# Moving the gate, the subtractions and the order of products in the head of a gated attention kernel

## The chip, the cores and the metric

The kernel runs on one core of a Trainium2 chip. The metric is the device time of one execution in microseconds; the time before is 2952.81 us, the median of three runs (2950.8 to 2952.96). The engines are called TensorE (PE in the profile), VectorE (DVE), ScalarE (ACT), GpSimd (POOL) and SyncE (SP), which issues nearly all DMA transfers from one queue in program order.

## The reference

For one sequence x of 2048 rows and 1024 columns, in fp32, with 32 heads of 32 columns:

```python
g = sigmoid((x * gate_w).sum(-1, keepdims=True))
a = linear_attention(x, A_wqkv, A_wo)      # phi(q), phi(k); num / den; @ wo
b = softmax_attention(x, B_wqkv, B_wo)     # softmax(q k^T / sqrt(32)) v; @ wo
return g * a + (1 - g) * b
```

Each attention begins with `x @ wqkv`, a 2048 x 1024 by 1024 x 3072 product. The gate `g` is one number for each row of x.

## The kernel before, in words

**Precision.** TensorE multiplies fp32 operands as a rounded high part and a remainder. `split` (L292) makes both: ScalarE copies the source to the high part (L293), and an engine given by the caller subtracts the high part from the source (L294). `three` (L148) then issues three matmuls (L152, L155, L157) for each pair of operands: high by high, and the two mixed ones.

**The head** is everything ahead of `linear()`. It computes the q, k and half of the v of the softmax attention, in two passes J over halves of the sequence. One pass has two parts.

*v.* `v_pass` (L397) goes over eight steps k of the contraction and adds 24 matmuls a step into all eight PSUM banks. The loop at L573 (pass 0) and the one at L629 (pass 1) feed it: x and weight tiles of 128x512 are loaded and split (`split_x`, `split_wv`). At the end `v_out` (L355) has ScalarE copy the eight banks to SBUF buffers (L356) and SyncE store them.

*q and k.* For these the kernel takes seven products instead of eight for a 2x2 block product (a Strassen-Winograd scheme). `sides` (L370) forms sums of x tiles, `split_sides` and `last_side` split them; `quad_weights` (L418) forms and splits seven weight combinations from four raw tiles. `quad` (L444) runs one group: seven products of 12 matmuls each into six banks taken in turn (`NQB`, `turns`), and combinations of them on VectorE (L468 to L482), which read the banks and leave four results. Each result is split by `store` (L458) and sent to DRAM (`qk_d`). There are eight groups in a pass (`QUADS`). `PRODUCTS` gives their order: X11, X21, X22 are pieces of x itself, T1 to T4 are sums; `PLACE` says which big buffers hold each.

**Order of work.** Within the head the program order is written out by hand: between two products `next(side)` advances several generators (`beside`, L505): the next group's weights one step, the late T4 splits (`late_side`), the spill of split x to DRAM (`spill_rest`), and one piece of the gate (`gate`, L491). Each engine runs its instructions in this order. A gate piece is a load of 128 rows by 256 columns of x into `kvb`, which is the only buffer for it, and a VectorE multiply with a sum (L497); there are 64, four for each of 16 row tiles. `leave` (L675), in the last group, begins the loads of the next stage.

**After the head**, `linear()` (L930) makes units of 24 matmuls: first the second half of v (16 units, one for each 128 rows), with x read back from DRAM (`load_half`), then the linear attention's k, v and q. A planner at L1637 interleaves the units with the softmax attention's heads by modelled engine times (`T`, `use`); row maxima of the first heads (L1126, L1131) run beside the second half of v. The weights of the next projection are split towards the end of a stage (`renew`, `split_w`: ScalarE L729, VectorE L731). From the heads on GpSimd adds up softmax rows (L1392).

Of the kernel before, what the change touches and what calls it, by code (L numbers as in the profile page):

```python
# [10 lines left out]
F32 = mybir.dt.float32  # L11
F32R = mybir.dt.float32r
AF = mybir.ActivationFunctionType
ALU = mybir.AluOpType
# [33 lines left out]
def kernel(  # L48
# [260 lines left out]
    PLACES = [dict(zip(SIDE, PLACE)), dict(zip(["X11", "T4", "X21", "X22", "T1", "T2", "T3"], PLACE))]  # L309
    for side in PLACES:  # L310
        side["X12"] = side["T4"]
    PRODUCTS = ["X11", "T1", "T2", "X21", "T3", "X22", "T4"]
# [37 lines left out]
    H11, H22, H12, H21, P1, U2, W2, C22 = mid[6], mid[7], mid[8], mid[9], mid[2], mid[10], mid[11], mid[12]  # L350
# [19 lines left out]
    def sides(raws, i):  # L370

        r11, r12, r21, r22 = raws
        nc.gpsimd.tensor_sub(r11, r12, r11)
        nc.gpsimd.tensor_sub(r12, r22, r12)
        nc.gpsimd.tensor_sub(r22, r22, r11)
        nc.gpsimd.tensor_sub(t4_raw[i], r21, r22)

    def split_sides(raws, J, i):
        r11, r12, _, r22 = raws
        for name, raw in (("T1", r11), ("T2", r22), ("T3", r12)):  # L380
            split(xpiece(J, name, 0, i), xpiece(J, name, 1, i), raw, nc.gpsimd)

    def last_side(J, parts):
        for i in parts:
            split(xpiece(J, "T4", 0, i), xpiece(J, "T4", 1, i), t4_raw[i], nc.vector if i % 2 else nc.gpsimd)

    def spill(J, name):

# [29 lines left out]
    def quad_weights(raws, J, f):  # L418

        w11, w12, w21, w22 = raws  # L420

        def part(s, raw, eng):
            n = quad_ring(J, f, s)
            split(ring_w(n, 0), ring_w(n, 1), raw, eng)

        part(0, w11, nc.gpsimd)
        part(6, w22, nc.vector)
        nc.vector.tensor_add(w22, w21, w22)
        nc.vector.tensor_sub(w21, w11, w21)
        yield  # L430
        part(1, w22, nc.gpsimd)
        nc.vector.tensor_sub(w11, w22, w11)
        yield
        part(3, w12, nc.gpsimd)
        part(2, w11, nc.vector)
        yield
        nc.vector.tensor_sub(w12, w12, w11)
        part(4, w21, nc.gpsimd)
        yield
        part(5, w12, nc.vector)  # L440

    turns = count()

    def quad(J, f, side):  # L444
# [12 lines left out]

        def store(i, jj, src, hi):  # L458
            split(f32r(hi), f32r(src), src, nc.gpsimd)
# [9 lines left out]
        nc.vector.tensor_add(W2, p5, U2)  # L469
        next(side, None)  # L470
        nc.vector.tensor_add(P1, product(3), P1)
        store(0, 0, P1, H11)
        next(side, None)
        p7 = product(4)
        nc.vector.tensor_add(C22, p7, W2)
        nc.vector.tensor_add(U2, p7, U2)
        store(1, 1, C22, H22)
        next(side, None)
        nc.vector.tensor_add(W2, product(5), W2)
        store(0, 1, W2, H12)  # L480
# [5 lines left out]
    GW = NK * DH  # L486
    NG = D // GW
    gate_x = kvb.rearrange("p k d -> p (k d)")
    tg = mx[0].rearrange("p t i -> p (t i)")

    def gate():  # L491
        dma(zrep, bass.AP(tensor=gate_w.tensor, offset=gate_w.offset, ap=[[0, P], [1, D]]))
        for t in range(NT):
            for i in range(NG):
                dma(gate_x, x[t * P:(t + 1) * P, i * GW:(i + 1) * GW])
                yield
                nc.vector.scalar_tensor_tensor(bank[7][:, :GW], gate_x, 1.0, zrep[:, i * GW:(i + 1) * GW],  # L497
                                               op0=ALU.mult, op1=ALU.mult, accum_out=tg[:, t * NG + i:t * NG + i + 1])
# [4 lines left out]
        nc.vector.tensor_scalar(omg_sb, g_sb, -1.0, 1.0, op0=ALU.mult, op1=ALU.add)  # L503

    def beside(*streams):  # L505

# [22 lines left out]
    for _ in range(WARM):  # L529
        nc.tensor.matmul(bank[7][:, :P], ones, ones, start=True, stop=True)  # L530

    gates = gate()
    V_BANKS = [list(range(8)), [6, 7, 2, 3, 4, 5, 0, 1]]
    raws_q = [raw_a, raw_b]

# [22 lines left out]

    def quads(J, first, spills):

        sides_ = [late_side(J), spills, gates]
        for f in range(QUADS - 1):
            if f + 2 < QUADS:
                load_quad(raws_q[f % 2], f + 2)
            else:
                first()
            quad(J, f, beside(quad_weights(raws_q[(f + 1) % 2], J, f + 1), *sides_))
# [26 lines left out]
        big[b] = big_tile(b, F32R)  # L594
    w_t[3] = big[RAW_BIG[0]]
    quad_w = quad_weights(raw_a, 0, 0)
    next(quad_w)
    next(quad_w)
    split_sides(raw_x0[3], 0, 3)
    load_quad(raw_b, 1)  # L600
    for _ in quad_w:
        pass
    for t in range(2 * TPC):
        v_out(0, t, bank[V_BANKS[0][t]], v_outs[t % 4])

    def change():

# [52 lines left out]
            for _ in quad_w:  # L660
                pass
    for t in range(2 * TPC):
        v_out(0, 2 * TPC + t, bank[V_BANKS[1][t]], v_outs[t % 4])

    def load_v1(raws, ks):
        for raw, k in zip(raws, ks):
# [252 lines left out]
        give(b, 0.0, [item])  # L919
        o_left.append(item)  # L920

    for s in [gates]:
        for _ in s:
            pass
    quad(1, QUADS - 1, leave())
    T["sp"] = 0.0
    for m in range(3):
# [1 line left out]

    def linear():  # L930
        extra = iter(())
        for n, (i, t) in enumerate(units):
            kind, c = chunks[i]
            follow = chunks[i + 1] if i + 1 < len(chunks) else None
# [787 lines left out]
```

## Time and profile before

| what | value |
|---|---|
| median of three runs | 2952.81 us |
| profiled execution | 2949.11 us, its span 2947.3 us |
| TensorE busy | 2848.4 us, 97% of the span |
| VectorE busy | 2204.3 us, 75% |
| ScalarE busy | 1598.0 us, 54% |
| GpSimd busy | 2170.3 us, 74% |
| mean granted TensorE clock | 0.984 |
| DMA | 428.57 MB, 139 GB/s of it to and from HBM |

Lines of windows give, for a stretch of the span in microseconds, its length and then the busy time of PE, of PE's weight loads, DVE, ACT and POOL (with the number of instructions), the granted PE clock, the busy share of the DMA engines and GB/s. Lines of waits give who waited for what: microseconds in total, times, longest. Lines of the timeline give start, length, engine, line, operation, and in brackets the idle time in front and what ended it. Neighbouring matmuls overlap, so a matmul's length is not the distance to the next.

### The profile page before, as it was taken

The numbers are of one execution on the slowest core, as the hardware profiler recorded it, in microseconds if no ns is written. First come the engines' busy times: TensorE is split into PE (matmuls) and PEld (weight loads), VectorE is DVE, ScalarE is ACT, GpSimd is POOL, SyncE is SP. The second block draws the span as 40 slices with busy tenths as digits, with TensorE's granted clock in tenths as the row PEclk, the third lists the DMA queues.
The fourth block names the chain that finished last, engine by engine and source line by source line (L and its number), as shares of the span: only waits on it lengthen the run. The fifth ranks groups of instructions, "written<-read, shape, count | busy, mean of one in ns | idle before, by whom it ended". The sixth has DMA issues, their size and how long they took to land.

```text
span 2947.3 us, 46931 instructions
## 1 busy us (share of the span) xinstructions
PE 2848.4 (97%) x15944; PEld 2070.4 (70%) x15944; DVE 2204.3 (75%) x3568; ACT 1598.0 (54%) x2994; POOL 2170.3 (74%) x1082
## 2 busy tenths in 40 slices
PE   8888789899999999999999999999999999999999
PEld 6667677777767767767776777777676667666787
DVE  6555465378888888888888888878887888787622
ACT  4223333046667666766676666666666666566410
POOL 7445555039999998999999999889989988886000
PEclk9889999999999999999999999999999999999999
DMA  7656675643334433433443335446666454643542
GB/s 237 208 177 205 190 221 190 208 158 101 100 98 126 110 91 98 128 101 100 106 125 91 97 99 145 141 152 192 187 182 207 130 154 121 176 117 113 198 158 79
DMA packets 383626, 428.57 MB, mean 145 GB/s; under 512 B 105774, under 2 KB 219694, under 8 KB 383388
## 3 DMA queue, kind: packets, MB, share of 16 engines
q1 hardware_dynamic: 369788, 412.47, 45.9%
q0 software_dynamic: 13600, 13.11, 3.3%
q8 instruction: 127, 2.08, 0.3%
q14 instruction: 111, 0.91, 0.1%
HBM read 298.06 MB, written 112.98 MB: 139 GB/s over the span
## 4 chain that ended last, share of the span: by engine, by line
PE 85%; DMA 4%; issue 1%; POOL 1%; DVE 1%; ACT 0%; SPq 0%; DVEq 0%; POOLq 0%; ACTq 0%
PE bank L1300 16%; PE bank L1126 16%; PE bank L1457 15%; PE bank L152 12%; PE bank L155 12%; PE bank L157 12%; DMA kvb<-in_x 2%; PE bank L1191 1%; PE bank L907 1%; DMA big<-wa 0%; PE bank L796 0%; DMA big<-wv 0%; SPq L169 0%; POOL big L294 0%; DMA big<-xs 0%
## 5 line engine op out<-in xcount | busy, mean ns | idle before, releaser
L1392 POOL TENSOR_TENSOR big<-big,big 128x512 f32<-128x512 f32 (+2 forms) x694 | 1644.7, 2374 | 118.8 <-ACT big L1303 76.1
L1131 DVE TENSOR_REDUCE mx<-bank 128x1 f32<-128x512 f32 x2048 | 1308.6, 683 | 318.5 <-PE bank L1126 314.6
L1303 ACT ACTIVATE big<-bank 128x512 f32<-128x512 f32 x2048 | 1180.2, 602 | 430.8 <-PE bank L1300 360.2
L1126 PE MATMUL bank<-big,big 128*128 128x512 f32 x1888 | 738.7, 392 | 4.8 <-DMA big<-qk 3.6
L1300 PE MATMUL bank<-big,big 128*128 128x512 f32 x1888 | 742.3, 394 | 0.5 <-ACT mid L356 0.5
L152 PE MATMUL bank<-big,big 128*128 128x512 f32 x1600 | 637.0, 398 | 73.7 <-DVE mid L469 32.7
L155 PE MATMUL bank<-big,big 128*128 128x512 f32 x1600 | 633.8, 396 | 6.4 <-POOL big L294 5.4
L157 PE MATMUL bank<-big,big 128*128 128x512 f32 x1596 | 631.0, 395 | 0.4 <-DVE big L294 0.4
L1457 PE MATMUL bank<-big,mid 128*32 128x512 f32 x4096 | 454.1, 593 | 0.0
L1300 PEld LDWEIGHTS bank<-big,big 128*128 128x128 f32 x1888 | 353.9, 188 | 126.8 <-issue 48.6
L1126 PEld LDWEIGHTS bank<-big,big 128*128 128x128 f32 x1888 | 354.3, 188 | 80.6 <-ACT big L1303 4.2
L152 PEld LDWEIGHTS bank<-big,big 128*128 128x128 f32 x1600 | 306.8, 192 | 146.7 <-issue 36.7
L155 PEld LDWEIGHTS bank<-big,big 128*128 128x128 f32 x1600 | 307.0, 192 | 72.2 <-POOL big L294 6.0
L157 PEld LDWEIGHTS bank<-big,big 128*128 128x128 f32 x1596 | 305.4, 191 | 65.7 <-DVE big L294 0.8
L1457 PEld LDWEIGHTS bank<-big,mid 128*32 128x32 f32 x4096 | 142.3, 110 | 265.5 <-issue 265.5
L1408 DVE TENSOR_TENSOR bank<-bank,big 128x512 f32<-128x512 f32 x364 | 251.8, 692 | 5.7 <-ACT big L1303 3.9
L294 POOL TENSOR_TENSOR mid<-mid,mid 128x512 fp32r<-128x512 f32 x64 | 83.4, 1304 | 164.6 <-ACT mid L293 164.5
L152 PE MATMUL bank<-big,xh 128*128 128x512 f32 x384 | 151.6, 395 | 6.4 <-DMA xh<-xs 5.6
L155 PE MATMUL bank<-big,xh 128*128 128x512 f32 x384 | 151.0, 393 | 0.7 <-DMA big<-wa 0.7
L157 PE MATMUL bank<-big,xh 128*128 128x512 f32 x384 | 150.6, 392 | 0.3 <-DMA xh<-xs 0.3
L1388 POOL TENSOR_TENSOR big<-big,big 128x1536 f32<-128x1536 f32 (+1 forms) x31 | 122.5, 3952 | 35.8 <-ACT big L1303 35.8
L293 ACT CAST mid<-mid 128x512 fp32r<-128x512 f32 x64 | 39.7, 621 | 180.1 <-issue 68.7
(129 smaller groups left out, 2111.6 us busy)
## 6 DMA issues: line engine op xcount, KB each, us to landing
big<-xs SPq DMA_DIRECT2D x300, 256.0 KB
big<-qk SPq DMA_DIRECT2D x720, 64.0 KB
xh<-xs SPq DMA_DIRECT2D x148, 256.0 KB
qk<-mid SPq DMA_DIRECT2D x128, 256.0 KB
big<-oA SPq DMA_DIRECT2D x84, 256.0 KB
xs<-big SPq DMA_DIRECT2D x64, 256.0 KB
oA<-mid SPq DMA_DIRECT2D x64, 256.0 KB
big<-big POOLq DMA_DIRECT2D x50, 256.0 KB, 5.6
```

What stands on the lines that cost most here:

```text
L152: yield nc.tensor.matmul(ps, sh, mh_, start=(kt == 0), stop=False)
L155: yield nc.tensor.matmul(ps, sh, ml_, start=False, stop=(late and last))
L157: yield nc.tensor.matmul(ps, sl, mh_, start=False, stop=last)
L294: eng.tensor_sub(lo, src, f32(hi))
L1126: nc.tensor.matmul(bank[b], q[:, t % TPC * P:(t % TPC + 1) * P], k[:, j * C:(j + 1) * C], start=True, stop=True)
L1131: nc.vector.tensor_reduce(m[:, t, j:j + 1], bank[b], AX.X, ALU.max)
L1300: nc.tensor.matmul(bank[b], k[:, t * P:(t + 1) * P], q_cols(h, j), start=True, stop=True)
L1303: nc.scalar.activation(pr_t[i][:, j * C:(j + 1) * C], bank[b], AF.Exp, scale=SCALE)
L1388: nc.gpsimd.tensor_add(lacc[:, :qp], pr(0)[:, :qp], pr(1)[:, :qp])
L1392: nc.gpsimd.tensor_add(lacc[:, sl], lacc[:, sl], pr(t)[:, sl])
L1408: nc.vector.tensor_add(lacc[:, qp:] if t == NT - 1 else l_b[:, :n], l_b[:, :n], src)
L1457: nc.tensor.matmul(av_b[j * DH:(j + 1) * DH, :], v[:, t, :], pr(t)[:, j * C:(j + 1) * C], start=(t == 0), stop=(t == NT - 1))
```

## The change

Four things change in the head, and one in the stage behind it:

- `split`'s subtraction, the sums of x in `sides` and the T4 splits all go to VectorE; GpSimd keeps none of them.
- The seven products come in the order X11, X21, X22, T1, T2, T3, T4, with `quad_weights` and the combinations reordered to match. The result that was in P1 with H11 is now in C11; P1 takes another result.
- The eight evictions of v rotate over six buffers (two of them halves of `zrep`) instead of four. The load of the second group's weights comes behind the first group's weights, not ahead of their last steps.
- The gate is no longer among the side generators. It loads a whole row tile (128 by 1024 columns, 512 KB) into one half of big buffer 12, two halves in turn, and multiplies it in one VectorE instruction, with a modelled cost of 1.2 us.
- `linear()` advances the gate once per unit of the second half of v, behind its fifth step, and twice in the last unit.

```diff
-    SIDE = ["X11", "T1", "T2", "X21", "T3", "X22", "T4"]
+    PRODUCTS = ["X11", "X21", "X22", "T1", "T2", "T3", "T4"]
...
-    t4_raw = [H22, C22, H12, H21]
-    v_outs = [P1, U2, W2, H11]
+    t4_raw = [H12, H22, H21, U2]
+    v_outs = [P1, C11, H11, W2] + halves(zrep)
...
-        nc.gpsimd.tensor_sub(r11, r12, r11)
+        nc.vector.tensor_sub(r11, r12, r11)
...
-            split(xpiece(J, name, 0, i), xpiece(J, name, 1, i), raw, nc.gpsimd)
+            split(xpiece(J, name, 0, i), xpiece(J, name, 1, i), raw, nc.vector)
...
         nc.vector.tensor_add(w22, w21, w22)
+        yield
         nc.vector.tensor_sub(w21, w11, w21)
+        part(1, w12)
         yield
-        part(1, w22, nc.gpsimd)
         nc.vector.tensor_sub(w11, w22, w11)
-        yield
-        part(3, w12, nc.gpsimd)
-        part(2, w11, nc.vector)
+        part(3, w22)
         yield
         nc.vector.tensor_sub(w12, w12, w11)
-        part(4, w21, nc.gpsimd)
+        part(4, w11)
         yield
-        part(5, w12, nc.vector)
+        part(2, w12)
+        yield
+        part(5, w21)
...
         nc.scalar.copy(P1, product(0))
         next(side, None)
-        p5 = product(1)
+        nc.vector.tensor_add(C11, product(1), P1)
+        store(0, 0, C11, H11)
         next(side, None)
-        nc.vector.tensor_add(U2, product(2), P1)
+        p3 = product(2)
+        next(side, None)
+        p5 = product(3)
+        next(side, None)
+        nc.vector.tensor_add(U2, product(4), P1)
         nc.vector.tensor_add(W2, p5, U2)
+        nc.vector.tensor_add(P1, p3, W2)
+        store(0, 1, P1, H12)
         next(side, None)
...
     def gate():
+        xn = halves_of(big_tile(12, F32))
+        junk = halves_of(big_tile(13, F32))[0]
         dma(zrep, bass.AP(tensor=gate_w.tensor, offset=gate_w.offset, ap=[[0, P], [1, D]]))
         for t in range(NT):
-            for i in range(NG):
-                dma(gate_x, x[t * P:(t + 1) * P, i * GW:(i + 1) * GW])
-                yield
-                nc.vector.scalar_tensor_tensor(bank[7][:, :GW], gate_x, 1.0, zrep[:, i * GW:(i + 1) * GW],
-                                               op0=ALU.mult, op1=ALU.mult, accum_out=tg[:, t * NG + i:t * NG + i + 1])
-        nc.vector.tensor_reduce(g_sb, tg.rearrange("p (t i) -> p t i", i=NG), AX.X, ALU.add)
+            dma(xn[t % 2], x[t * P:(t + 1) * P, :])
+            yield
+            use("dve", 1.2)
+            nc.vector.scalar_tensor_tensor(junk, xn[t % 2], 1.0, zrep, op0=ALU.mult, op1=ALU.mult,
+                                           accum_out=g_sb[:, t:t + 1])
...
-        sides_ = [late_side(J), spills, gates]
+        sides_ = [late_side(J), spills]
...
                 store_mix()
+                if kind == "v" and k == NK // 2:
+                    next(gates, None)
+                    if t == NT - 1:
+                        next(gates, None)
```

More of the change, by code (lines that the diff above doesn't have):

```diff
@@ L307 @@
     PLACE = [(4, 5), (8, 9), (10, 11), (12, 13), (0, 1), (2, 3), (6, 7)]
[L308 to L309 removed]
+    PRODUCTS = ["X11", "X21", "X22", "T1", "T2", "T3", "T4"]
+    PLACES = [dict(zip(PRODUCTS, PLACE)), dict(zip(["X11", "T4", "X21", "X22", "T1", "T2", "T3"], PLACE))]
     for side in PLACES:
         side["X12"] = side["T4"]
[L312 removed]
     NQB = 6
@@ L349 @@
     raw_x1 = [raw_a, raw_b, raw_a, raw_b]
-    H11, H22, H12, H21, P1, U2, W2, C22 = mid[6], mid[7], mid[8], mid[9], mid[2], mid[10], mid[11], mid[12]
-    t4_raw = [H22, C22, H12, H21]
-    v_outs = [P1, U2, W2, H11]
+    H11, H22, H12, H21, P1, U2, W2, C11 = mid[6], mid[7], mid[8], mid[9], mid[2], mid[10], mid[11], mid[12]
+    t4_raw = [H12, H22, H21, U2]
+    v_outs = [P1, C11, H11, W2] + halves(zrep)
     wv_d = [dram.tile([P, 2 * C], F32, name=f"wv{k}") for k in range(NK)]
@@ L372, in sides @@
         r11, r12, r21, r22 = raws
-        nc.gpsimd.tensor_sub(r11, r12, r11)
-        nc.gpsimd.tensor_sub(r12, r22, r12)
-        nc.gpsimd.tensor_sub(r22, r22, r11)
-        nc.gpsimd.tensor_sub(t4_raw[i], r21, r22)
+        nc.vector.tensor_sub(r11, r12, r11)
+        nc.vector.tensor_sub(r12, r22, r12)
+        nc.vector.tensor_sub(r22, r22, r11)
+        nc.vector.tensor_sub(t4_raw[i], r21, r22)
     def split_sides(raws, J, i):
@@ L380, in split_sides @@
         for name, raw in (("T1", r11), ("T2", r22), ("T3", r12)):
-            split(xpiece(J, name, 0, i), xpiece(J, name, 1, i), raw, nc.gpsimd)
+            split(xpiece(J, name, 0, i), xpiece(J, name, 1, i), raw, nc.vector)
     def last_side(J, parts):
         for i in parts:
-            split(xpiece(J, "T4", 0, i), xpiece(J, "T4", 1, i), t4_raw[i], nc.vector if i % 2 else nc.gpsimd)
+            split(xpiece(J, "T4", 0, i), xpiece(J, "T4", 1, i), t4_raw[i], nc.vector)
     def spill(J, name):
@@ L420, in quad_weights, with part @@
         w11, w12, w21, w22 = raws
-        def part(s, raw, eng):
+        def part(s, raw):
             n = quad_ring(J, f, s)
-            split(ring_w(n, 0), ring_w(n, 1), raw, eng)
-        part(0, w11, nc.gpsimd)
-        part(6, w22, nc.vector)
+            split(ring_w(n, 0), ring_w(n, 1), raw, nc.vector)
+        part(0, w11)
+        part(6, w22)
         nc.vector.tensor_add(w22, w21, w22)
+        yield
         nc.vector.tensor_sub(w21, w11, w21)
+        part(1, w12)
         yield
-        part(1, w22, nc.gpsimd)
         nc.vector.tensor_sub(w11, w22, w11)
-        yield
-        part(3, w12, nc.gpsimd)
-        part(2, w11, nc.vector)
+        part(3, w22)
         yield
         nc.vector.tensor_sub(w12, w12, w11)
-        part(4, w21, nc.gpsimd)
+        part(4, w11)
         yield
-        part(5, w12, nc.vector)
+        part(2, w12)
+        yield
+        part(5, w21)
     turns = count()
@@ L458, in store @@
         def store(i, jj, src, hi):
-            split(f32r(hi), f32r(src), src, nc.gpsimd)
+            split(f32r(hi), f32r(src), src, nc.vector)
             j = 2 * J + jj
@@ L465, in quad @@
         next(side, None)
-        p5 = product(1)
+        nc.vector.tensor_add(C11, product(1), P1)
+        store(0, 0, C11, H11)
         next(side, None)
-        nc.vector.tensor_add(U2, product(2), P1)
+        p3 = product(2)
[3 more added lines that the diff above has]
+        nc.vector.tensor_add(U2, product(4), P1)
         nc.vector.tensor_add(W2, p5, U2)
+        nc.vector.tensor_add(P1, p3, W2)
+        store(0, 1, P1, H12)
         next(side, None)
[L471 to L475, printed above, removed]
+        p7 = product(5)
+        nc.vector.tensor_add(W2, p7, W2)
         nc.vector.tensor_add(U2, p7, U2)
[L477 to L480, printed above, removed]
+        store(1, 1, W2, H22)
         next(side, None)
@@ L503, in gate, with halves_of @@
         nc.vector.tensor_scalar(omg_sb, g_sb, -1.0, 1.0, op0=ALU.mult, op1=ALU.add)
+    def halves_of(t):
+        return [t[:, i * D:(i + 1) * D] for i in range(2)]
     def beside(*streams):
@@ L530 @@
         nc.tensor.matmul(bank[7][:, :P], ones, ones, start=True, stop=True)
-    gates = gate()
     V_BANKS = [list(range(8)), [6, 7, 2, 3, 4, 5, 0, 1]]
@@ L596 @@
     quad_w = quad_weights(raw_a, 0, 0)
-    next(quad_w)
-    next(quad_w)
+    for _ in range(3):
+        next(quad_w)
     split_sides(raw_x0[3], 0, 3)
-    load_quad(raw_b, 1)
     for _ in quad_w:
         pass
+    load_quad(raw_b, 1)
     for t in range(2 * TPC):
-        v_out(0, t, bank[V_BANKS[0][t]], v_outs[t % 4])
+        v_out(0, t, bank[V_BANKS[0][t]], v_outs[t % len(v_outs)])
     def change():
@@ L662 @@
     for t in range(2 * TPC):
-        v_out(0, 2 * TPC + t, bank[V_BANKS[1][t]], v_outs[t % 4])
+        v_out(0, 2 * TPC + t, bank[V_BANKS[1][t]], v_outs[t % len(v_outs)])
     def load_v1(raws, ks):
@@ L920, in queries @@
         o_left.append(item)
-    for s in [gates]:
-        for _ in s:
-            pass
     quad(1, QUADS - 1, leave())
@@ L931, in linear @@
         extra = iter(())
+        gates = gate()
         for n, (i, t) in enumerate(units):
```

4 lines of the change are left out of this document (removed).

## The prediction

> **What bounds the kernel now.** I read the page first, then the stages as windows, then TensorE's waits, then single stretches of the timeline.
>
> ```profile
> span 2947.3 us, 46931 instructions
> PE 2848.4 (97%) x15944; PEld 2070.4 (70%) x15944; DVE 2204.3 (75%) x3568; ACT 1598.0 (54%) x2994; POOL 2170.3 (74%) x1082
> PE   8888789899999999999999999999999999999999
> ```
>
> TensorE is busy nine tenths or more from slice 9 on; only the first 600 us have holes. The windows are the stages of that head: first half of v, eight groups of products, second v pass, three groups, five groups, the change-over, and the second half of v.
>
> ```profile
> core 0: us, PE busy (x) PEld busy (x) DVE busy (x) ACT busy (x) POOL busy (x), PEclk, DMA share, GB/s
> 4.70:49.60 44.90, 44.89 (x193) 36.69 (x192) 39.92 (x27) 20.36 (x37) 38.95 (x25) 1.00 0.89 289
> 62.10:265.30 203.20, 167.81 (x672) 134.77 (x673) 111.01 (x207) 58.16 (x104) 78.95 (x60) 0.90 0.62 194
> 265.30:312.40 47.10, 46.59 (x192) 37.24 (x192) 18.78 (x14) 14.54 (x26) 40.89 (x30) 0.95 0.49 169
> 325.80:400.50 74.70, 63.37 (x252) 50.99 (x253) 37.16 (x73) 21.97 (x40) 28.07 (x21) 0.91 0.70 212
> 400.50:498.70 98.20, 98.20 (x421) 81.06 (x422) 62.19 (x77) 37.63 (x66) 53.15 (x40) 0.97 0.62 207
> 540.00:628.00 88.00, 86.45 (x380) 70.52 (x378) 51.76 (x77) 11.44 (x20) 0.00 (x0) 1.00 0.66 208
> ```
>
> A group of seven products is 84 matmuls (x672 is eight groups). With the gate beside them eight groups take 203.2 us, 25.4 each; five after the gate has ended take 98.2 us, 19.6 each, without a hole. So the gate, not the products, paces the first eleven.
>
> ```profile
> PE bank L152 <- DVE mid L469: 32.7, 8, 7.2
> PE bank L152 <- ACT mid L356: 25.9, 2, 13.4
> PE bank L152 <- DMA big<-wv: 5.5, 1, 5.5
> ```
>
> ```profile
> L169 SPq DMA_DIRECT2D kvb<-in_x x64: 328/338/872, 73.7 to 393.3; - x64
> L497 DVE SCALAR_TENSOR_TENSOR bank<-kvb,zrep x64: 419/434/1515, 79.0 to 397.3; 128x256 f32<-128x256 f32 x64
>   DMA kvb<-in_x: 100.4, 56
> ```
>
> VectorE stands 100.4 us, 56 times, for a gate piece in the single buffer `kvb`; L469, the read that frees the bank which the next group's first product needs, comes behind it in VectorE's order. The other large waits are the two evictions of v (L356).
>
> ```profile
> 49.20 0.39 PE L157 MATMUL bank<-big,big 128*128 128x512 f32 x1
> 62.12 0.79 PE L152 MATMUL bank<-big,big 128*128 128x512 f32 x1 [12.54 <-ACT mid L356]
> 82.03 0.50 PE L155 MATMUL bank<-big,big 128*128 128x512 f32 x1 [1.03 <-DVE big L294]
> 84.77 0.50 PE L152 MATMUL bank<-big,big 128*128 128x512 f32 x1 [2.00 <-ACT big L293]
> 87.97 0.79 PE L155 MATMUL bank<-big,big 128*128 128x512 f32 x1 [2.70 <-POOL big L294]
> 138.45 0.77 PE L152 MATMUL bank<-big,big 128*128 128x512 f32 x1 [7.20 <-DVE mid L469]
> 139.01 0.63 PE L155 MATMUL bank<-big,big 128*128 128x512 f32 x1
> 518.58 0.80 PE L152 MATMUL bank<-big,big 128*128 128x512 f32 x1 [6.23 <-DMA big<-xs]
> 531.71 0.80 PE L152 MATMUL bank<-big,xh 128*128 128x512 f32 x1 [5.62 <-DMA xh<-xs]
> ```
>
> ```profile
> 400.50:406.50 6.00, 6.00 (x14) 4.72 (x15) 5.35 (x8) 2.70 (x5) 4.17 (x3) 0.51 0.40 131
> ```
>
> A long wait costs twice: behind one, 400.50 to 406.50 is run at a granted clock of 0.51 and starts 14 matmuls, where 98.20 us for 421 (0.233 each) would start 26: some 2.8 us lost.
>
> **The change part by part.** Floor of the head first. Five groups in 98.2 us, less the 2.8 us of slow clock at their start, give 19.07 us a group and 0.227 a matmul; the first v pass takes 44.9 us, the second would take 43.6 (192 matmuls). Together 44.9 + 16 x 19.07 + 43.6 = 393.6 us, where the head now takes 494.0, from 4.7 to 498.7 (end of the fifth group). So 100.4 us are to be had, no more.
>
> *Subtractions to VectorE.* About 190 POOL instructions of the head become VectorE's. What one costs depends on POOL:
>
> ```profile
> 334.42 0.69 DVE L428 TENSOR_TENSOR mid<-mid,mid 128x512 f32<-128x512 f32 x1
> 73.65 1.74 DVE L432 TENSOR_TENSOR mid<-mid,mid 128x512 f32<-128x512 f32 x1
> 73.55 4.38 POOL L294 TENSOR_TENSOR big<-mid,big 128x512 fp32r<-128x512 f32 x3 [2.00 <-DMA extra<-in_b_wqkv]
> 118.19 1.37 DVE L294 TENSOR_TENSOR big<-extra,big 128x512 fp32r<-128x512 f32 x1 [0.66 <-ACT big L293]
> L294 DVE TENSOR_TENSOR big<-mid,big 128x512 fp32r<-128x512 f32 (+2 forms) x57 | 62.8, 1111 | 58.5 <-ACT big L293 50.3 <-DMA v<-mid 8.0
> ```
>
> The same 128x512 subtraction takes 0.69 us while POOL is idle and 1.74 us inside a POOL run; L294's mean of 1.11 us mixes both. After the change POOL has nothing in the head, so I take 0.69, and keep 1.11 as the far end. Per group VectorE then has 7 bank reads, 4 store subtractions, 7 weight subtractions and 4 weight sums: 22 x 0.69 = 15.2 us. Four store subtractions wait for a ScalarE cast just ahead (0.66 us each; one is covered by other work), so 15.2 + 2.0 = 17.2 us in 19.07: VectorE is nearly full but not the bound. It runs some 3 us late; the tightest bank, the third product's, is read 16 us into a group and needed again at 22. Loss: 0, up to 1 us a group.
>
> First v pass: 13 subtractions per two steps, 9.0 us beside 10.9 us of TensorE.
> ```profile
> 10.30 2.40 DVE L294 TENSOR_TENSOR big<-xh,big 128x512 fp32r<-128x512 f32 x2 [1.37 <-ACT big L293]
> 61.49 1.07 ACT L356 COPY mid<-bank 128x512 f32<-128x512 f32 x2
> ```
>
> The second step's first tiles are split from 10.30 us on. From there VectorE has some 44 operations to the end of the pass and 14 for the first group's weights: 40 us, so done near 50. ScalarE's casts run ahead of it, and the evictions start about then instead of at 61.49: the 12.54 us wait shrinks to about 1 us. The second pass begins with VectorE some 8 us late (twelve more operations in the last group), 43 operations of 0.69 us and two reloads of x deep; I expect 2 us at its start, where the last bank is freed late, and 2 us of the 13.37 at its end. The reload of v's weights (5.5 us) was late because SyncE stood behind gate loads; it goes.
>
> *Order of products.* The first three use pieces of x itself, so sums of x are wanted eight us later. That relieves the first group (1.03, 2.00 and 2.70 us above, at T4); four late splits remain in front of its last product: 1 us. The single P1 is new: its store leaves after the fifth product, and ScalarE's copy of the next group's first product must wait for it. From that store back to itself there are 15 VectorE operations (10 us), casts and copies (2.5 us) and the store's issue and landing (4 to 5 us): 17 to 18 us, under 19.07. Free, if the store lands in 6 us.
>
> With 1 us for early v steps and 2 us of slow clock the leftover is 1 + 2 + 2 + 1 + 1 + 2 = 9 us: the head shortens by 91, to 403 us.
>
> [...]
>
> *The gate in the second half of v.* 64 loads of 128 KB become 16 of 512 KB on SyncE's queue, with the 512 KB weight load ahead, one per tile between two loads of x; 64 multiplies of 0.434 + 0.14 us become 16 of 1024 columns. That length is not in the trace: four times the old would be 2.3 us, the slope from 256 (0.43) to 512 (0.69) gives 1.2 us, which I take, since the fixed part isn't paid four times. 16 x 1.35 = 22 us of VectorE, in a stage where it is busy 51.8 of 88 us: covered. The last tile isn't: two multiplies run in one step, the second on a load issued just before it, and the weight splits for the next projection and ScalarE's casts queue behind it.
> ```profile
> 91.89 0.60 SPq L169 DMA_DIRECT2D kvb<-in_x  x1
> 96.22 0.43 DVE L497 SCALAR_TENSOR_TENSOR bank<-kvb,zrep 128x256 f32<-128x256 f32 x1 [3.85 <-DMA kvb<-in_x]
> ```
>
> A 128 KB piece is there 4.3 us after its issue; 512 KB takes perhaps 2 us more, less the multiply in front, so VectorE stands about 5 us. TensorE has three steps of this tile and two of the next before it needs the third split (5 x 0.68 = 3 us): 2 us lost, with a slow start behind it 5. Covered: 0; the whole stand and a slow start: 9.
>
> For the loads: the stage moves 208 GB/s at a share of 0.66. 8.9 MB more over some 105 us is 85 GB/s, a share of 0.26 at the 324 GB/s of the last row below. With 0.92, and loads of x two halves ahead (6 us), it should hold: 2 us. At the change-over it is worse:
>
> ```profile
> 512.54 2.68 SPq L169 DMA_DIRECT2D big<-xs  x4
> 515.75 10.98 SPq L169 DMA_DIRECT2D big<-qk  x18
> 527.45 1.75 SPq L169 DMA_DIRECT2D xh<-xs  x2
> 518.50:522.00 3.50, 3.42 (x8) 2.72 (x9) 0.00 (x0) 0.00 (x0) 0.00 (x0) 0.50 1.04 324
> ```
>
> The queue is full (share 1.04 at 324 GB/s) and 1 MB of gate goes in front of the loads for which TensorE now waits 5.62 us: 1 MB at 324 GB/s is 3.2 us, with issue 4. Gate in all +11 (0 to 28: sixteen 512 KB loads at that rate, 1.6 us each, wholly exposed, are 26).
>
> Sum: 2949.1 us (span 2947.3 and 1.8 around it) - 91 + 11 = 2869; the median of the runs lies 3.7 us above that execution, so 2873.
>
> **The rivals.** (1) *The gate's loads starve v.* All 26 us exposed, and the last tile's 9: 2873 + 24 = 2897. For it: share 0.66 already. Against: TensorE stands 1.5 us in those 88.
>
> (2) *A loop in the group is longer than the products:* P1's store or the casts; at 21 us a group 16 x 1.9 = 31 us: 2904. For it: 17.2 of 19.07 us booked, stores up to 0.85 us each to issue on SyncE behind four weight loads. Against: without the gate's loads SyncE stands less.
>
> (3) *Slower: VectorE stays slow without POOL.* At 1.11 us an operation a group needs 22 x 1.11 + 2 = 26.4 us, more than today's 25.4: 16 groups are 422 us against 203 + 75 + 98 = 376 now; +46, the v waits give back 20 and the gate costs 11: 2990. It decides from about 1.0 us an operation. Against it: each slow operation I looked at lies inside a POOL run. [...]
>
> (4) *More is gained:* the gate hidden, leftovers nothing: 2949 - 100 + 4 = 2853.
>
> **How the numbers follow.** Forecast (2860 to 2888) 0.60; rivals 1 and 2, 0.13 each; rival 3, 0.05; rival 4, 0.07; no net change 0.02. The range 2853 to 2908 takes in 1, 2 and 4 and leaves the rest out. A measurement of this kernel tells 0.2% (6 us) from nothing. Faster 0.93, same 0.02, slower 0.05.
>
> **What would show it.** Right: no wait for L469's counterpart, groups of 19 us throughout, VectorE's L294 near 0.69 us, POOL idle until the heads, second half of v beginning near 408 us instead of 499, and a new wait near its end. Wrong: L294 above 1 us; groups of 21 us with waits on the store of P1; loads of x late all through the second half of v.

## The result and the profile after

The changed kernel takes 2866.28 us (median of four, 2866.01 to 2867.1) where the kernel before, measured beside it, takes 2951.81 (2949.71 to 2952.96): a ratio of 0.9712, 95% interval 0.9695 to 0.9728. The profiled execution is the 2866.15 us one, with a span of 2864.4 us; its counterpart before is 2949.11. The prediction was 2873, range 2853 to 2908, so the sign and the likeliest case were right and the time came out 7 us lower.

The page of the changed kernel shows where: TensorE has no slice under eight tenths, and GpSimd, apart from a few memsets, begins at the heads.

```profile
span 2864.4 us, 46550 instructions
PE 2825.9 (99%) x15944; PEld 2058.1 (72%) x15944; DVE 2233.2 (78%) x3659; ACT 1595.8 (56%) x2994; POOL 1909.2 (67%) x894
PE   9999988899999999999999999999999999999999
POOL 0000010299999999999999999889889888885000
```

The head as windows (columns as in the windows of before): first v pass and all eight groups in one, second v pass with the other eight, the change-over, and the second half of v with the gate in it.

```profile
core 0: us, PE busy (x) PEld busy (x) DVE busy (x) ACT busy (x) POOL busy (x), PEclk, DMA share, GB/s
4.70:206.60 201.90, 201.90 (x886) 166.49 (x885) 152.10 (x239) 83.62 (x150) 0.00 (x0) 1.00 0.79 250
211.00:404.00 193.00, 193.00 (x844) 159.66 (x845) 138.41 (x217) 76.73 (x136) 8.57 (x7) 0.99 0.68 213
404.00:442.00 38.00, 20.87 (x73) 15.36 (x73) 8.48 (x14) 2.37 (x5) 2.25 (x2) 0.80 0.79 224
442.00:544.00 102.00, 92.81 (x400) 74.65 (x398) 65.89 (x109) 11.50 (x22) 0.00 (x0) 0.97 0.82 275
```

TensorE is busy for all of the first 201.90 us and all of the 193.00 us of the second window: 886 matmuls at 0.228 us and 844 at 0.229, the 0.227 that the prediction took from the undisturbed groups of before. Of the sixteen groups none has a hole. All that is left stands between those windows and behind them. These are TensorE's waits in the first 600 us (total, times, longest) and their places in the timeline:

```profile
PE bank L152 <- DMA xh<-xs: 10.5, 2, 9.5
PE bank L1301 <- ACT mid L355: 7.9, 1, 7.9
PE bank L152 <- DMA big<-xs: 5.2, 2, 4.5
PE bank L152 <- DVE mid L483: 4.3, 1, 4.3
PE bank L1127 <- DMA big<-qk: 2.8, 1, 2.8
```

```profile
211.00 0.50 PE L152 MATMUL bank<-big,big 128*128 128x512 f32 x1 [4.32 <-DVE mid L483]
414.97 1.85 PE L1127 MATMUL bank<-big,big 128*128 128x512 f32 x7 [2.82 <-DMA big<-qk]
421.35 0.80 PE L152 MATMUL bank<-big,big 128*128 128x512 f32 x1 [4.53 <-DMA big<-xs]
439.60 0.80 PE L152 MATMUL bank<-big,xh 128*128 128x512 f32 x1 [9.49 <-DMA xh<-xs]
544.46 0.79 PE L1301 MATMUL bank<-big,big 128*128 128x512 f32 x1 [7.91 <-ACT mid L355]
```

The 32.7 us of waits for L469, the 25.9 for the evictions and the 5.5 for the reload of v's weights are gone; so are the three at T4. The head, from 4.7 us to the end of the fifth group of pass 2, takes 399.3 us where it took 494.0. Its end, 404.0, is worked out: TensorE runs without a hole to 412.15, where the 2.82 us wait begins, and the last 36 matmuls of that run, at 0.2267 us, are the next stage's.

### The profile page after: what moved, and what is told of

Read it like the earlier page. It is cut to its first block, busy times and chain, and to the rows that moved or that the text cites. A ratio compares the mean times of both kernels' runs of the same rounds, so it can differ in the third digit from the quotient of the medians.

```text
span 2864.4 us, 46550 instructions
## 1 busy us (share of the span) xinstructions
PE 2825.9 (99%) x15944; PEld 2058.1 (72%) x15944; DVE 2233.2 (78%) x3659; ACT 1595.8 (56%) x2994; POOL 1909.2 (67%) x894
## 4 chain that ended last, share of the span: by engine, by line
PE 90%; DMA 2%; SPq 0%; DVE 0%; ACT 0%; issue 0%; ACTq 0%; DVEq 0%
PE bank L1301 17%; PE bank L1127 16%; PE bank L1458 16%; PE bank L152 13%; PE bank L155 13%; PE bank L157 13%; PE bank L1192 1%; PE bank L906 1%; DMA big<-wa 0%; PE bank L795 0%; DMA big<-xs 0%; DMA xh<-xs 0%; SPq L169 0%; DMA big<-qk 0%; PE bank L1184 0%; DMA big<-in_x 0%
```

## The experiments

The theory is that of the prediction: in the head two things each made TensorE wait, the gate's 64 pieces in VectorE's order, and subtractions slowed by GpSimd; with both gone TensorE runs through, and what is left lies in the first steps of pass 2, at the change-over and in the last tile of the gate. Each kernel below was timed beside the kernel before, and its ratio is to that.

**Only the gate moved.** The kernel before, with the gate of the changed kernel in its new place.

```diff
-        sides_ = [late_side(J), spills, gates]
+        sides_ = [late_side(J), spills]
...
+                if kind == "v" and k == NK // 2:
+                    next(gates, None)
+                    if t == NT - 1:
+                        next(gates, None)
```

> The kernel before, with nothing but the gate moved as in the changed kernel. Theory (the gate paces the groups of products): the groups fall to 19.1 us each, because five groups without the gate ran so before, and the late reload of v's weights (5.5 us) goes; the two waits for the evictions of v (12.5 and 13.4 us) and those for T4 (5.7 us) stay. From the windows of before: 203.2 + 74.7 us for eleven groups less 11 x 19.07 is 68 us, less the 5.7 us at T4 and 2 us of slow clock there, and 7.8 us for the reload with its slow clock: 68 us less in the head, 12 us more in the second half of v: 56 us faster, 2896 us. Rival (VectorE and GpSimd slowing each other paces the groups): less than 20 us faster.

Measured: 2892.86 us, ratio 0.9813 (0.9797 to 0.983). The waits for the bank reads are gone, and the groups from 84.50 us on run without a hole (a window, then a line of TensorE's waits); the two evictions stay:

```profile
84.50:260.00 175.50, 175.50 (x775) 145.10 (x775) 98.01 (x110) 62.15 (x109) 110.65 (x82) 1.00 0.63 203
```

```profile
PE bank L152 <- ACT mid L356: 24.0, 2, 12.5
```

So GpSimd's subtractions did not pace the groups: with GpSimd busy 110.65 of these 175.50 us TensorE still has no hole. The gate did. One thing went otherwise than expected: at T4, where 5.7 us of waits were to stay, 1.70 us are left (at 84.00).

**The gate put back.** The changed kernel, with the old gate among the side generators.

```diff
-        sides_ = [late_side(J), spills]
+        sides_ = [late_side(J), spills, gates]
...
-        v_out(0, 2 * TPC + t, bank[V_BANKS[1][t]], v_outs[t % len(v_outs)])
+        v_out(0, 2 * TPC + t, bank[V_BANKS[1][t]], v_outs[t % 4])
```

> The changed kernel with the gate put back into the head as it was before (64 pieces in one buffer, beside the products); the second pass evicts v over four buffers instead of six, because the gate's weights lie in the other two. Theory: the gate's pieces pace the groups again, at 25 us or more (VectorE now has 22 subtractions and sums and seven pieces in each group), while the evictions of v stay short: 2866 - 12 + 68 = 2922 us, up to 2940 if the pieces wait behind the subtractions. Rival (freeing VectorE from GpSimd is what shortened the groups): within 15 us of the changed kernel.

Measured: 2915.63 us, ratio 0.9889 (0.9874 to 0.9904), some 6 us under what was expected. The group waits are back although VectorE's subtractions stay fast (waits of TensorE; then the group of VectorE's L294 from 5 to 400 us, with count, busy us, mean ns, and idle time in front):

```profile
PE bank L152 <- DVE mid L475: 37.8, 8, 7.0
```

```profile
L294 DVE TENSOR_TENSOR big<-mid,big 128x512 fp32r<-128x512 f32 (+1 forms) x92 | 60.5, 682 | 22.7 <-ACT big L293 22.7
```

L475 is the counterpart of L469: eight waits again, 37.8 us in place of 32.7. A VectorE whose operations take 682 ns does not help while it stands for gate pieces.

**Subtractions back on GpSimd.** The changed kernel, with the old engines in `sides`, `split_sides`, the weights, the T4 splits and the stores.

```diff
-            split(f32r(hi), f32r(src), src, nc.vector)
+            split(f32r(hi), f32r(src), src, nc.gpsimd)
...
-        nc.vector.tensor_sub(r11, r12, r11)
+        nc.gpsimd.tensor_sub(r11, r12, r11)
```

> The changed kernel with the subtractions put back on GpSimd where it had them before (sums of x, their splits, half of T4, the stores, and weight parts 0, 1, 3 and 4). Theory: the groups stay at 19.1 us, since without the gate they have room, but the evictions of v wait again for the chain of GpSimd and VectorE: 12 and 13 us and 4 us of slow clock come back, 2 to 6 us at the second pass's start may change: 2866 + 28 = 2894 us. Rival (the gate is the whole of the gain): 2866 to 2872 us.

Measured: 2898.77 us, ratio 0.9831 (0.9816 to 0.9846), some 5 us above what was expected. The evictions wait again, VectorE's subtraction takes twice as long, and TensorE stands 4.4 us at T4, for a split on GpSimd:

```profile
PE bank L152 <- ACT mid L355: 19.1, 2, 12.2
PE bank L155 <- POOL big L294: 4.4, 1, 4.4
```

```profile
L294 DVE TENSOR_TENSOR big<-mid,big 128x512 fp32r<-128x512 f32 (+1 forms) x40 | 57.2, 1440 | 70.5 <-ACT big L293 67.6 <-DMA qk<-mid 2.7
```

**Gate and VectorE, without the order.** The first experiment with every subtraction on VectorE: old order of products, old four eviction buffers.

```diff
-            split(xpiece(J, name, 0, i), xpiece(J, name, 1, i), raw, nc.gpsimd)
+            split(xpiece(J, name, 0, i), xpiece(J, name, 1, i), raw, nc.vector)
...
-            split(f32r(hi), f32r(src), src, nc.gpsimd)
+            split(f32r(hi), f32r(src), src, nc.vector)
```

> The kernel before with the gate moved and all subtractions on VectorE, but the old order of products, the old order of weights and four eviction buffers: the changed kernel without its order of products. Theory (the order is worth only the waits for T4 in the first group and a few us at the evictions): 2866 to 2876 us. Rival (the order carries the evictions' gain too, as the weight parts come earlier): 2885 us or more.

Measured: 2865.68 us, ratio 0.9718 (0.9703 to 0.9732), where the changed kernel has 0.9712 (0.9695 to 0.9728): the order of products and the two more buffers are worth nothing that can be measured; the intervals leave room for some 5 us either way. These are all the waits of TensorE in its first 410 us but one of 1.1 at the start of the kernel:

```profile
PE bank L152 <- DVE mid L482: 4.1, 1, 4.1
PE bank L152 <- ACT big L293: 1.1, 1, 1.1
```

So the T4 waits did not need the new order: most of them went with the gate (1.70 us left in the first experiment), the rest with GpSimd, and with GpSimd they come back in the new order too (4.4 us in the third experiment). With GpSimd subtracting, the new order is no faster than the old either (2898.77 against 2892.86 us, with intervals that meet). On one chip, then: 2949 before, 2893 with the gate moved, 2866 with VectorE besides. The gate is worth 56 us net, the engine 27. Alone, VectorE and the order gave 33 (the second experiment). These 33 and the gate's 56 make 89 against 83 together; both remove the 5.5 us wait for the reload of v's weights (the first has none left, the second one of 0.5 us) and part of the waits at T4, which would count them twice; that these make up the whole difference is not shown.

**No gate at all.** The changed kernel with `g` set to a constant.

```diff
-            dma(xn[t % 2], x[t * P:(t + 1) * P, :])
-            yield
-            use("dve", 1.2)
-            nc.vector.scalar_tensor_tensor(junk, xn[t % 2], 1.0, zrep, op0=ALU.mult, op1=ALU.mult,
-                                           accum_out=g_sb[:, t:t + 1])
...
+        yield
+        nc.vector.memset(g_sb, 0.5)
+        nc.vector.memset(omg_sb, 0.5)
```

> The changed kernel with the gate left out of the computation: its 17 loads and 16 multiplies are gone and g is set to 0.5, so the mix of the two attentions is not the reference's. It measures what the gate costs in the second half of v. Theory: all that the change loses behind the head (waits and slow clock of 29.5 us from the fifth group of the second pass to the end of v, against 20 before) is the gate's: 2866 - 11 = 2855 us. Rival (v's loads stand because the head now drains faster into the change-over): 2863 us or more.

Measured: 2854.01 us, ratio 0.9677 (0.9662 to 0.9691): behind the head the gate costs 12.3 us by the medians, some 10 us by the ratios. The end of the stage loses its 7.91 us wait, and the third wait of the change-over is 2.4 us shorter, not gone:

```profile
436.64 0.80 PE L152 MATMUL bank<-big,xh 128*128 128x512 f32 x1 [7.06 <-DMA xh<-xs]
```

**Loads a tile earlier.** What does the 7.91 us wait at 544.46 hang on? The timeline of the changed kernel at the end of the stage (SPq is SyncE's queue; the number behind the start is the time to issue):

```profile
526.78 0.44 SPq L169 DMA_DIRECT2D big<-in_x  x1
532.58 1.23 DVE L495 SCALAR_TENSOR_TENSOR big<-big,zrep 128x1024 f32<-128x1024 f32 x1 [3.58 <-DMA big<-in_x]
534.54 0.33 SPq L169 DMA_DIRECT2D big<-in_x  x1
540.38 1.23 DVE L495 SCALAR_TENSOR_TENSOR big<-big,zrep 128x1024 f32<-128x1024 f32 x1 [6.57 <-DMA big<-in_x]
541.64 0.22 ACT L497 ACTIVATE g_sb<-g_sb 128x16 f32<-128x16 f32 x1 [13.37 <-DVE big L495]
543.83 0.57 ACT L355 COPY mid<-bank 128x512 f32<-128x512 f32 x1
544.46 0.79 PE L1301 MATMUL bank<-big,big 128*128 128x512 f32 x1 [7.91 <-ACT mid L355]
```

Each of the last two loads is used 5.8 us after its issue, and VectorE stands 3.58 and 6.57 us for them. ScalarE stands for VectorE at L497, and the copy that frees the bank which TensorE needs next (L355) comes behind that in ScalarE's order. If this is the chain, loads issued two tiles ahead take the wait away:

```diff
+        for t in range(2):
+            dma(xn[t], x[t * P:(t + 1) * P, :])
         for t in range(NT):
-            dma(xn[t % 2], x[t * P:(t + 1) * P, :])
             yield
...
+            if t + 2 < NT:
+                dma(xn[t % 2], x[(t + 2) * P:(t + 3) * P, :])
```

> The changed kernel with the gate's row tiles loaded two steps ahead instead of one, so the last multiply doesn't follow its own load. Theory: the stand of VectorE (6.6 us) in the last tile and TensorE's wait of 7.9 us behind it go, with the slow clock after it: 2866 - 8 = 2858 us; the change-over may lose 1 to 2 us, with one more load in its full queue. Rival (the queue is full at the end of v, and the splits wait for their weights anyway): 2863 us or more.

Measured: 2859.79 us, ratio 0.9698 (0.9684 to 0.9712). The wait behind L355 is 0.4 us now; 6.5 us less by the medians, while the ratio's interval still meets that of the changed kernel.

**Three mends together.** The loads ahead; the gate's first multiply at the third tile, away from the change-over; and the next sums of x moved behind the read of the last bank, against the 4.32 us at 211.00.

```diff
+        yield
         sides(raw_x1[0], 0)
...
-                if kind == "v" and k == NK // 2:
-                    next(gates, None)
-                    if t == NT - 1:
-                        next(gates, None)
+                if kind == "v" and k == NK // 2 and t >= 2:
+                    for _ in range(2 if t in (5, 8, 11) else 1):
+                        next(gates, None)
```

> Three repairs on the changed kernel: the gate's loads two steps ahead, the gate begun at the third tile of the second half of v instead of the first (three later tiles take two steps), and in the last group of the first pass the sums of x moved behind the read of the last bank. Theory: 8 us at the last tile, 4 us of the 9.5 at the change-over, and 4.3 us of wait with 2 of slow clock at the start of the second v pass: 2866 - 18 = 2848 us. Rival (the waits move on: a later split in the second v pass, a later tile of v): 2855 us or more.

Measured: 2848.44 us, ratio 0.9658 (0.9641 to 0.9674), clear of the changed kernel by 18 us. The second v pass starts without a wait, so the 4.32 us had the cause that the timeline of the changed kernel names:

```profile
208.45 0.69 DVE L375 TENSOR_TENSOR mid<-xh 128x512 f32<-128x512 f32 x1 [3.08 <-DMA qk<-mid]
210.26 0.68 DVE L483 TENSOR_TENSOR mid<-bank,mid 128x512 f32<-128x512 f32 x1
```

VectorE stands 3.08 us at a sum of x that overwrites H12, until H12's store has landed, and L483, the read of the last bank, is queued behind it. At the change-over the mended kernel still waits 6.07 us:

```profile
415.46 10.84 SPq L169 DMA_DIRECT2D big<-qk  x18
427.01 1.78 SPq L169 DMA_DIRECT2D xh<-xs  x2
431.50 0.79 PE L152 MATMUL bank<-big,xh 128*128 128x512 f32 x1 [6.07 <-DMA xh<-xs]
```

**The eighteen loads of the second head.** Two theories for that wait. By order: the load of x is issued late because 18 small loads hold SyncE for 10.84 us. By bytes: the queue is full, and whatever stands with those loads waits. The first was mine. Moving them three tiles on should remove the wait by the first, and only move it by the second.

```diff
-            if n == 1:
+            if n == 4:
                 load_head(1)
                 load_v(1)
```

> The kernel with the three repairs, and the loads of the second head's q, k and v issued with the fifth tile of the second half of v instead of the second. Theory: what is left at the change-over is the queue: 18 small loads take SyncE 10.8 us there, ahead of the load of x for which TensorE waits 6.1 us with some 2 us of slow clock; without them the wait goes: 2848 - 7 = 2841 us. Rival (the queue's bytes, not its order, set that wait, or the 18 loads stand in the way of a later tile): 2846 us or more.

Measured: 2851.84 us, ratio 0.9671 (0.9655 to 0.9687). The wait went with the burst, and grew:

```profile
434.48 0.47 PE L152 MATMUL bank<-big,xh 128*128 128x512 f32 x1 [2.14 <-DMA xh<-xs]
435.55 10.73 SPq L169 DMA_DIRECT2D big<-qk  x18
447.00 1.80 SPq L169 DMA_DIRECT2D xh<-xs  x2
451.48 0.80 PE L152 MATMUL bank<-big,xh 128*128 128x512 f32 x1 [8.23 <-DMA xh<-xs]
```

In both kernels the load of x for which TensorE stands is issued right behind the burst (427.01 and 447.00) and used 4.5 us later; here the load that was held before is issued at 415.26, and nothing waits for it. Yet the burst brings its bytes along wherever it stands, so the wait alone does not part the two theories. The same loads, then, in seven parts, one to a tile:

```diff
-            if n == 1:
-                load_head(1)
-                load_v(1)
+            if 1 <= n <= 7:
+                (lambda: load_k(1, 0), lambda: load_q(1, 0), lambda: load_k(1, 1), lambda: load_k(1, 2),
+                 lambda: load_k(1, 3), lambda: load_q(1, 1, NJ), lambda: load_v(1))[n - 1]()
```

> The kernel with the three repairs, and the second head's 18 loads and its load of v given out in seven parts, one with each of the second to the eighth tile of v, instead of in one row at the second. Theory (what TensorE waits for is the 10.7 us for which the 18 issues in a row hold SyncE's queue, wherever they stand): in parts of 3 they take 1.8 us a tile, no load of x waits for them, and the 6.1 us wait with its slow clock goes: 2848 - 7 = 2841 us. Rival (the bytes of x, head and gate together are too many for the DMA engines in these tiles): 2846 us or more.

Measured: 2847.26 us (2842.91 to 2849.86), ratio 0.9645 (0.9627 to 0.9663): not told apart from the three mends. The wait is split into five, the two largest being

```profile
427.48 1.60 SPq L169 DMA_DIRECT2D xh<-xs  x2
436.00 0.47 PE L152 MATMUL bank<-big,xh 128*128 128x512 f32 x1 [2.94 <-DMA xh<-xs]
450.61 0.80 SPq L169 DMA_DIRECT2D xh<-xs  x2
458.31 0.74 PE L152 MATMUL bank<-big,xh 128*128 128x512 f32 x1 [2.52 <-DMA xh<-xs]
```

Each line of TensorE is shown behind the issue of the load of x for which it stands. The DMA engines are busy for a share of 0.96 in this stretch (a window, columns as above):

```profile
436.00:466.00 30.00, 26.05 (x100) 19.36 (x101) 9.57 (x16) 1.76 (x3) 0.00 (x0) 0.94 0.96 303
```

No burst holds these two loads, and still they come 8.5 and 7.7 us after their issue, where behind a burst it was 4.5. The sum of the waits for x is some 7 us (2.94, 2.52 and three of 0.72, 0.36 and 0.30) where the mended kernel has 6.07 in one. So neither theory carries alone. The order is what held the load of x in the kernels with a burst; the kernel without the gate, which has the same burst and moves fewer bytes, has a wait of the same kind, 7.06 us.

With the burst gone something else makes the loads late, and what it is was not shown. The bytes fit: both loads are issued right behind loads of the gate (1.5 MB from 425.70 us on, 1 MB at 448.98), and so is the one for which the run before this waits 2.14 us (426.70, used 7.8 us later). No run moved these loads of the gate alone. Nor is this trace the whole of it: it is of an execution of 2849.75 us, and two of the four took 2842.91 and 2844.77 us, near the 2841 that the order had promised.

**What slows VectorE.** The prediction's rival 3 hung on GpSimd slowing VectorE. Two kernels give GpSimd work of no use in the changed kernel's first v pass and first groups, for the same 157 us: subtractions, which read and write, and memsets, which only write. The eviction buffers lose the half of `zrep` that this work uses.

```diff
-    v_outs = [P1, C11, H11, W2] + halves(zrep)
+    v_outs = [P1, C11, H11, W2, halves(zrep)[1]]
...
+    scr = zrep[:, :C]
+    nc.gpsimd.memset(scr, 0.0)
+    for _ in range(120):
+        nc.gpsimd.tensor_sub(scr, scr, scr)
```

> The changed kernel with 120 subtractions on GpSimd ahead of everything, of a 128x512 scratch tile from itself, which nothing waits for (the evictions of v use five buffers, the sixth is the scratch). Theory (VectorE's subtraction of 0.69 us takes 1.1 to 1.7 while GpSimd reads SBUF): during GpSimd's run, some 160 to 200 us, L294 on VectorE takes 1.1 us or more, the first eviction of v comes 25 us later or more, groups in the run take 25 us or more, and the rest is as before: 2920 to 2950 us. Rival (VectorE was slow beside GpSimd for another reason, the chain of casts): L294 stays at 0.69 us and the time at 2866.

In the second kernel the loop is

```diff
+    for _ in range(300):
+        nc.gpsimd.memset(scr, 0.0)
```

> As the run before this with subtractions on GpSimd, but with 300 fills of the scratch tile in their place: GpSimd is busy for about 160 us (0.53 us each) and only writes SBUF. Theory (what slows VectorE's two-input subtraction is GpSimd's reading): L294 stays near 0.69 us and the time is 2866 us, up to 2870. [...] Rival (any GpSimd instruction on SBUF slows VectorE): L294 above 0.9 us and 2890 us or more.

Measured, two timed executions each: 2932.09 us, ratio 0.9941 (0.9922 to 0.9961), with the subtractions; 2863.6 us, 0.9709 (0.969 to 0.9728), with the memsets. Groups by line of the first kernel, GpSimd's work and VectorE's subtraction beside it (5 to 180 us; by its 157.5 us of work and 9.3 of idle time GpSimd's run ends near 168, so a few of the 31 are free of it), then the latter from 200 to 400 us, when GpSimd is idle:

```profile
L532 POOL TENSOR_TENSOR zrep<-zrep 128x512 f32<-128x512 f32 x120 | 157.5, 1312 | 9.3
L294 DVE TENSOR_TENSOR big<-mid,big 128x512 fp32r<-128x512 f32 (+1 forms) x31 | 41.1, 1351 | 6.4 <-ACT big L293 6.3
```

```profile
L294 DVE TENSOR_TENSOR big<-mid,big 128x512 fp32r<-128x512 f32 x59 | 39.0, 686 | 15.0 <-ACT big L293 15.0
```

and of the second (VectorE from 5 to 160 us):

```profile
L532 POOL MEMSET zrep<- 128x512 f32 x300 | 157.9, 526 | 17.2
L294 DVE TENSOR_TENSOR big<-mid,big 128x512 fp32r<-128x512 f32 (+1 forms) x42 | 27.8, 683 | 11.6 <-ACT big L293 11.6
```

Beside GpSimd's subtractions VectorE's takes 1351 ns (22 others of the same window, of the form `big<-big,big`, take 1488), beside an idle GpSimd 686, beside its memsets 683. So it is not that GpSimd is busy, which it is for 157.5 and 157.9 us. The two kinds of work differ in that one reads; no run parts the reading from the rest of a subtraction. The windows of the first kernel give rival 3's picture while it lasts and the changed kernel's after it:

```profile
60.00:200.00 140.00, 108.04 (x419) 85.23 (x420) 123.06 (x120) 39.73 (x73) 102.40 (x79) 0.84 0.57 178
200.00:400.00 200.00, 195.69 (x856) 161.56 (x855) 143.84 (x226) 77.20 (x136) 0.00 (x0) 0.99 0.71 222
```

VectorE is busy 123.06 of 140 us and TensorE starts 419 matmuls, three in 1.00 us; afterwards 856 in 200, 4.3 in a microsecond. (The first window holds some 30 us behind the end of GpSimd's run, so the picture is rather too mild.)

## Why the prediction was right, point by point

**Floor of the head.** 393.6 us was the sum of undisturbed stages. The changed kernel needs 399.3, of which 4.32 us are the wait at 211.00 and the rest its slow clock and small change. The head shortened by 94.7 us; the forecast was 91.

**Subtractions at 0.69 us.** The means of L294 with VectorE alone are 681 and 693 ns, in these groups of the first 404 us:

```profile
L294 DVE TENSOR_TENSOR big<-mid,big 128x512 fp32r<-128x512 f32 (+1 forms) x112 | 73.8, 681 | 30.9 <-ACT big L293 30.9
L294 DVE TENSOR_TENSOR mid<-mid,mid 128x512 fp32r<-128x512 f32 x62 | 42.9, 693 | 36.3 <-ACT mid L293 34.2
```

So 22 operations fit in a group, rival 3 did not come (its 1.11 us were a mean that took in the time beside a subtracting GpSimd), and nothing was lost in the groups, as taken. The loop over P1 and its store, rival 2, left no wait.

**The nine microseconds left over.** They came to 5.7. The first eviction of v, the second, T4, the early v steps: 1, 2, 1 and 1 us taken, none measured. The start of pass 2 was taken at 2 us and cost 4.32, with a slow clock behind it. The place was right and the cause only in part: the prediction had VectorE late there by the number of its operations, and the trace has it standing 3.08 us for the store of H12, a landing that the prediction had booked for P1 alone.

**Order of products.** The text gave it the relief at T4. The runs show that relief without the order, by the gate and VectorE; the order did nothing measurable. That step was wrong, at a size (5.7 us of waits) that the other steps paid: the sum did not suffer, by luck.

**The gate, +11.** Measured +10 to +12 by the kernel without it. Its terms: the multiply of 1024 columns at 1.2 us, by the slope from 256 to 512, takes 1.23; four times the old duration would have been 2.3. The change-over was taken at 4 and came to 3: 16.8 us of waits (2.82, 4.53, 9.49) where before has 15.5 (3.61, 6.23, 5.62), and some 5.7 us of slow clock behind them where before has 4.2 (146 matmuls in 38.87 us of busy time from 404 to 460 us, and 182 in 45.50 from 498.7 to 560, each at 0.227 us if undisturbed). Loads during the tiles, 2, cost next to nothing: TensorE stands 1.0 and 0.7 us for loads of x between 442 and 544 us, where the prediction counted 1.5 in the same stage of before. The DMA share is 0.82 (0.92 was estimated), and rival 1 did not come. The last tile was taken at 5 and came to some 10, past the bound of 9: 7.91 us of wait, and behind it 18 matmuls in 6.54 us where 29 fit, some 2.5 us lost. The prediction let one of the two multiplies stand, and both did, 3.58 and 6.57 us. The landing at 6 us was right (5.8). What it missed was who stands behind VectorE: it named the weight splits and ScalarE's casts for them, and it was ScalarE's activation at L497 with a bank copy behind it. So the +11 came out nearly right as a sum of terms that were off both ways, which is luck.

**The clock.** The window behind the one long wait of the head:

```profile
211.00:217.00 6.00, 6.00 (x19) 4.82 (x20) 5.22 (x9) 3.54 (x7) 0.00 (x0) 0.72 0.64 178
```

After 4.32 us of standing, 19 matmuls start at a granted clock of 0.72 where 26 fit, some 1.6 us lost. No run shows the 2 us of slow clock that the prediction took for the leftover waits; these 1.6 us, behind the one wait that was left, are what the runs have in their place. Shorter waits go both ways: behind 2.82 us here (at 414.97) and 2.72 us before (at 349.35) the granted clock is 1.00 in the first 2 us, behind 3.31 us before (at 373.13) it is 0.50, and so it is behind the 2.70 us at 87.97 which two other waits, of 1.03 and 2.00 us, precede.

**The sum.** The time of rival 4, 2853, which had nothing left over and the gate hidden, was reached only with the three mends. Against the profiled execution it was 2869, and 2866.15 was measured: the head 3.7 us better, the gate about as forecast. The other 4 us of the difference are the step from that execution to the median, taken at 3.7 us from before, where the changed kernel has 0.1. That step was scatter between executions: the medians of the kernel before, timed again beside the runs above, go from 2948.88 to 2951.81 us.

## What to carry to other kernels

Ask of each piece of side work what stands behind it in the order of its engine, and not what it costs: 64 multiplies of half a microsecond cost some 66 to 68 us of TensorE (56 net, and 10 to 12 given back behind the head), and the trace has VectorE standing for their loads into a single buffer, in front of the read that frees a bank. (A second buffer in the old place is a cheaper mend that no run tried.) Count an operation at the speed that its neighbours leave it (VectorE's subtraction took 0.68 us alone here, and 1.44 with the subtractions back on GpSimd), and look for that speed in a stretch of the trace where the neighbour is idle. At the end of a stage, see that the last loads are issued as far ahead as those in the middle, and follow who is queued behind the last wait: here two tiles of lead took a wait of 7.9 us down to 0.4 (6.5 us by the medians), and three mends of waits together were worth 18.

## What was not expected of the hardware

- GpSimd's subtractions, back to back, slow VectorE's from 0.69 to 1.35 us in the mean (1.49 in another group of 22 of them), while its memsets leave it at 0.68, although they keep GpSimd as busy (157.5 and 157.9 us).
- Spreading 18 loads, most of them of 64 KB, over seven tiles did not shorten, in the traced execution, the waits that their burst had made: at a DMA share of 0.96 the waits were cut up (2.94, 2.52 and three below 1 us) and not removed.
- A load of x comes 4.5 us after its issue when it is issued behind that burst, and 7.7 and 8.5 us after it in that stretch of the spread kernel; what sets the difference stays open.
